# Transposes moved from TensorE to DMA and more GELU chunks on VectorE, in a fused attention and MoE kernel

## The chip, the cores and the metric

The kernel runs on one core of a Trainium2 chip. Its engines are TensorE (PE in the profile; its weight loads are PEld), ScalarE (ACT), VectorE (DVE), GpSimd (POOL) and SyncE (SP), which here only issues DMAs. The metric is the device time of one execution in microseconds, as the median of several runs. Lower is better.

## The reference

Two stages, one after the other, for B = 4 batches, 12288 queries each, C = 128 channels:

```python
kv_pool = kv.reshape(B, H // 4, 4, W // 4, 4, C).mean(axis=(2, 4))   # 768 pooled rows per batch
k = v = kv_pool.reshape(B, -1, C) @ w_sr
a = softmax(q @ k.T / sqrt(C))                                       # 12288 x 768 per batch
x = (a @ v).reshape(49152, 128)
h = x @ w_in                                                         # 128 -> 2048
out = (h * sigmoid(1.702 * h)) @ w_out                               # 2048 -> 128
```

Inputs and output are float32; the kernel multiplies in bfloat16 and accumulates in float32.

## The kernel before

**Units.** Queries go in groups of 512 (`G`), 96 of them (`NG`); group `i` belongs to batch `i // 24`. A batch has 768 keys, 6 chunks of 128 (`JC`). The MoE has 16 chunks of 128 hidden channels per group (`FCH`). The unit of work is a chunk: 128 keys (or hidden channels) by 512 queries.

**Two rounds.** The kernel does attention for groups 0 to 47, the first MoE for them, attention for groups 48 to 95, the second MoE. Each stage is a stream of fills and drains. A fill is up to three matmuls of 128x512 into three banks of PSUM, then one ACTIVATE over all of them (exp or GELU), which writes weights in bfloat16 into `ag`, a store of 102 chunks in SBUF. A drain multiplies stored chunks by the values (128x129 matmuls, the last column being the sum) or by `w_out` (128x512). Two sets of three banks alternate between fills (`banks` 0, 1, 2 and 3, 4, 5); banks 6 and 7 (`acc`) serve everything else: accumulators of drains, transposes, keys, single chunks.

**A planner orders everything.** The code runs a list of fills (`seq`) with a list of drains (`todo`) and places drains and extra jobs between fills by a model of time in units of one 512-column matmul (`COST`, `now`, `end`, `dve`). The result is a fixed order of instructions on each engine; each engine runs in order and waits on semaphores. `background(i)` and `background_moe(g)` are called when the first fill of a group is prepared, up to two fills ahead of the drains that stand beside it, and issue loads and stores that belong to that moment. `extras` is a queue of small jobs that the planner fits in.

**Chunks on VectorE.** Some chunks skip ScalarE: `early_fill` makes one 128x512 matmul into bank 6 or 7 and VectorE computes exp or GELU by a polynomial and, for GELU, a reciprocal, into `aside` (three slots in rotation). `rolling` names the exp chunks, `lent` the GELU chunks, `early` four groups (48 to 51) whose 24 exp chunks are made during the first MoE. `raw`, a float32 copy of the chunk that GELU needs, lives in one of the four buffers of `qT`.

```python
rolling = [(i, JC - 1) for i in [10, *range(38, NG // R, 6), *range(57, 90, 6)]]
lent = [(g, FCH - 1) for g in range(52, 94) if g % 5 in (2, 4)]
```

That is 9 exp chunks beside the 24 early ones, and 17 GELU chunks, all in the second MoE.

**Queries.** Groups 0 to 11 are loaded with a cast into SBUF (`load_q`, on POOL's queue), and TensorE transposes them, four 128x128 transposes per group (`transpose_q`, L236), with a copy by VectorE (L242). All others are cast to DRAM (`cast_q`, POOL) and read back transposed by DMA (`load_qT`, SP), 2048 queries at a time.

**Keys and values.** Batches 0 and 1 are pooled by TensorE in the first attention stage. Batches 2 and 3 are pooled by eight pairs of accumulating DMAs (`add_kv`, POOL), started at groups 2 to 9 and 24 to 31 of the first MoE. Then, for each half `a` of a batch, at groups 12 and 14 (34 and 36), `use_kv` adds the last two terms on VectorE (`sum_kv`) and queues three jobs: `transpose_pooled` (four 96-row transposes on TensorE, L184, and a copy, L186), `make_k` (one 384-column matmul, L192, and a copy) and `make_v` (three 128-column matmuls, L199, and a copy, L201).

**Queues.** SP carries, in this order of mention only, the transposed query reads, the put-away of attention results to DRAM (`put_away`, 768 KB or 2 x 384 KB), their transposed return (`bring_back`), and the outputs (`out_dram<-o_sb`, four DMAs of 64 KB per group). `x`, `qT` and `o_sb` names in the profile are these tiles; `o_sb` has three buffers.

Of the kernel before, what the change touches and what calls it, by code (L numbers as in the profile page):

```python
# [7 lines left out]
F32 = mybir.dt.float32  # L8
# [16 lines left out]
def kernel(  # L25
# [23 lines left out]
    q_flat = q.rearrange("b n c -> (b n) c")  # L49
    x_bf = nc.dram_tensor("x_bf", (B * N, C), BF, kind="Internal").ap()  # L50
    q_bf = nc.dram_tensor("q_bf", (B * N, C), BF, kind="Internal").ap()

    kv_r = kv.rearrange("b (ch p) (a w) c -> b a ch p (w c)", p=128, a=2)

# [65 lines left out]
    def new_keys(b):  # L120
        kTs[b] = kvres.tile([128, J], BF, name="kT")

        vs[b] = kvres.tile([128, JC, C + 8], BF, name="v")
        nc.vector.memset(vs[b][:, :, C:C + 1], 1.0)

    def load_chunk(b, jc):
# [51 lines left out]
        pooled[b, a] = kvtmp.tile([Hp, 4, C], BF, name="pooled")  # L178
        nc.vector.tensor_tensor(pooled[b, a], t[:, 0], t[:, 1], ADD)

    def transpose_pooled(b, a):
        ps = acc_bf()[:, 0:h].rearrange("p (a b) -> p a b", a=4)
        for wp in range(4):
            nc.tensor.transpose(ps[:, wp, :], pooled[b, a][:, wp, :], ident[:Hp, :Hp])  # L184
        pTs[b, a] = kvtmp.tile([128, h], BF, name="pT")
        nc.vector.tensor_copy(pTs[b, a], ps.rearrange("p a b -> p (a b)"))  # L186

    def make_k(b, a):
        ps = acc()
        if a == 0:  # L190
            new_keys(b)
        nc.tensor.matmul(ps[:, :h], w_sr_sb, pTs[b, a], start=True, stop=True)  # L192
        nc.vector.tensor_copy(kTs[b][:, a * h:(a + 1) * h], ps[:, :h])

    def make_v(b, a):
        ps = acc()
        pT = pTs.pop((b, a))
        for k in range(K):
            nc.tensor.matmul(ps[:, k * C:(k + 1) * C], pT[:, k * 128:(k + 1) * 128], w_sr_sb,  # L199
                             start=True, stop=True)  # L200
        nc.vector.tensor_copy(vs[b][:, a * K:(a + 1) * K, 0:C], ps[:, :h].rearrange("p (k c) -> p k c", k=K))  # L201
        for jc in range(a * K, a * K + K):
            vs[b, jc] = True

    qTs = {}

    def cast_q(s):
        sl = slice(s * SG, (s + 1) * SG)
        nc.gpsimd.dma_start(out=q_bf[sl, :].rearrange("(p i) c -> p (i c)", p=128),
                            in_=q_flat[sl, :].rearrange("(p i) c -> p (i c)", p=128))  # L210

    def load_qT(s):
        qTs[s] = qpool.tile([128, 1, SG], BF, name="qT")
        nc.vector.memset(qTs[s][:, 0, 0:1], 0.0)
        nc.sync.dma_start_transpose(out=qTs[s], in_=q_bf[s * SG:(s + 1) * SG, :])


    QS = 3
    qs = [x_tile(XS - 1 - JC - s) for s in range(QS)]
# [8 lines left out]
    def transpose_q(g):  # L228
        s = g // 4
        turned.add(g)  # L230
        if g % 4 == 0:
            qTs[s] = qpool.tile([128, 1, SG], BF, name="qT")
        ps = acc_bf()[:, 0:G].rearrange("p (i t) -> p i t", i=4)
        for i in range(4):
            o = (g % 4) * G + i * 128
            nc.tensor.transpose(ps[:, i, :], qs[s][:, o:o + 128], ident)  # L236
        dst = qTs[s][:, 0, (g % 4) * G:(g % 4 + 1) * G].rearrange("p (t i) -> p t i", i=4)
        src = ps.rearrange("p i t -> p t i")
        if g == 0:
            nc.scalar.copy(dst, src)  # L240
        else:
            nc.vector.tensor_copy(dst, src)  # L242
# [10 lines left out]
    for jc in range(2, JC):  # L253
        load_chunk(0, jc)
    load_q(1, 2, 4)
    for s in range(2, QS):
        load_q(s, 0, 2)
        load_q(s, 2, 4)
    cast_q(3)
    cast_q(4)  # L260

# [66 lines left out]
        return K * len(free_frames())  # L328

    early = range(NG // R, NG // R + EARLY)  # L330
    rolling = [(i, JC - 1) for i in [10, *range(38, NG // R, 6), *range(57, 90, 6)]]
    lent = [(g, FCH - 1) for g in range(52, 94) if g % 5 in (2, 4)]
    aside = agpool.tile([128, K, 512], BF, name="aside")

    def weights(c):
        if c[0] == "a" and c[1] in early:
            return ag[:, (c[1] - early[0]) * JC + c[2], :]
        if c[0] == "a" and c[1:] in rolling:
            return aside[:, rolling.index(c[1:]) % K, :]
        if c[0] == "m" and c[1:] in lent:  # L340
            return aside[:, (len(rolling) + lent.index(c[1:])) % K, :]
        return ag[:, slot_of[c], :]


# [56 lines left out]
    COEFFS = (1.0000001192092896, -0.6931469440460205, 0.24022120237350464, -0.05550713464617729, 0.009675541892647743, -0.001327647129073739)  # L401

    def early_fill(i, jc):
        nonlocal steps, raw
        ps = acc()
        if (i, jc) in lent:
            if raw is None:
                raw = qpool.tile([128, 1, SG], BF, name="qT")[:, 0, 0:2 * G].bitcast(F32)
            nc.tensor.matmul(ps, w_in_sb[:, jc * 128:(jc + 1) * 128],  # L409
                             x[:, i % (4 * XS) * G:(i % (4 * XS) + 1) * G], start=True, stop=True)  # L410
            steps = lent_gelu(ps, weights(("m", i, jc)))
            early_step()
            return
        rhs = qTs[i // 4][:, 0, (i % 4) * G:(i % 4 + 1) * G]
        nc.tensor.matmul(ps, kTs[i // GB][:, jc * 128:(jc + 1) * 128], rhs, start=True, stop=True)  # L415
        steps = early_exp(ps, weights(("a", i, jc)))
        early_step()

    def early_step():
        nonlocal steps  # L420
# [58 lines left out]
    raw = None  # L479
    made, used = {}, []  # L480
    steps, early_todo = None, [c for c in rolling if c[0] < early[0]]
    early_todo += [(i, jc) for i in early for jc in range(JC)]
    early_todo += [c for c in rolling if c[0] > early[-1]] + lent

    def early_fits(p, i, jc):
        if (i, jc) in rolling:
            group = seq[p][1][0][0] if seq[p][0] == "a" else seq[p][1][0][0] // (NG // R) * (NG // R) + NG // R - 1
            return (i // GB, jc) in vs and (i in turned or i // 4 in qTs and i // 4 - 1 <= group // 4 and i >= 4 * QS) and len(used) > rolling.index((i, jc)) - K
        if (i, jc) in lent:
            return seq[p][0] == "m" and seq[p][1][0][0] >= i - 2 and len(used) > len(rolling) + lent.index((i, jc)) - K  # L490
        return low and min(slot_of.values()) >= low and (2, JC - 1) in vs

    def early_waits(t):
# [26 lines left out]
        nc.vector.memset(one, 0.0)  # L520
        nc.gpsimd.memset(one, 0.0)  # L521

    TURN = {6: 3, 7: 4, 8: 5, 20: 6, 21: 7, 22: 8, 25: 9, 32: 10, 35: 11, 40: 12}
    CAST = {0: [5], 13: [6], 14: [7], 15: [8], 16: [9], 26: [10, 11], 27: [12]}
    CAST_MOE = {20: 13, 21: 14, 22: 15, 23: 16, 33: 17, 34: 18, 35: 19, 36: 20, 37: 21, 38: 22, 39: 23}

    def background(i):

        first_round = i < GB * 2
        s = TURN.get(i, NS) if first_round else i // 4 + 3 if i % 4 == 0 else NS  # L530
        if s < NS:
            load_qT(s)
        if i in CAST:
            gate()
            for s in CAST[i]:
                cast_q(s)
        if i in (10, 12):
            gate()
            for jc in range(i % 10 * 3 // 2, i % 10 * 3 // 2 + 3):
                load_chunk(1, jc)  # L540
        if 0 <= i - 16 < JC:
            extras.append((key_and_value, 1, i - 16))
        if 0 <= i - 15 < JC:
            extras.append((pool_chunk, 1, i - 15))
        if i in (28, 33, 38):
            put_away(0, (i - 28) // 5)
        if i in (31, 36, 41):
            bring_back(0, (i - 31) // 5)
        if i == 28:
            gate()  # L550
            nc.gpsimd.dma_start(out=w_in_sb, in_=moe_w_in)
        if i == 29:
            gate()
            nc.gpsimd.dma_start(out=w_out_sb, in_=moe_w_out.rearrange("(o p) c -> p o c", p=128))

    def background_moe(g):
# [4 lines left out]
        if n == 0 and FIRST <= m < RT // PART:  # L561
            (bring_back if odd else put_away)(n, m)
        g += n * 4 * XS
        nonlocal low
        if g == 12:
            low = EARLY * JC
            order[:] = [f for f in order if f >= low // K]
# [3 lines left out]
        if g in (41, 42):  # L571
            load_qT(g - 28)
        if g == 43:
            background(early[0])
        for b, lo in ((2, 2), (3, 24)):
            if lo <= g < lo + 8:
                gate()
                add_kv(b, g - lo)
            if g in (lo + 10, lo + 12):
                use_kv(b, (g - lo - 10) // 2)  # L580

    def use_kv(b, a):
        nonlocal extra_at
        sum_kv(b, a)
        on_dve(3.5)
        extra_at = max(extra_at, dve + 1.5)
        extras.extend([(transpose_pooled, b, a), (make_k, b, a), (make_v, b, a)])

    extras = []

# [120 lines left out]
    def prepare(p):  # L711
# [3 lines left out]
        for i, jc in part:  # L715
# [22 lines left out]
        15: [(pool_chunk, 0, 5)],  # L738
        16: [(key_and_value, 0, 5), (later, 6)],
        17: [(later, 7)],  # L740
        18: [(later, g) for g in range(8, 12)]}

# [1 line left out]
    FIXED, CHUNK, SWITCH, HANDOVER, EVACUATE = 0.295, 1.978, 6.0, 1.0, 4.5  # L746
    COST = {pool_chunk: (1.9, 2.6), key_chunk: (0.3, 2.4), value_chunk: (0.3, 2.4),
            transpose_q: (1.05, 4.2), early_fill: (1.0, 5.5), key_and_value: (0.55, 3.5),
            transpose_pooled: (0.9, 3.6), make_k: (0.8, 3.2), make_v: (0.8, 3.7)}
    COPY = {pool_chunk: 1.5, key_chunk: 1.5, value_chunk: 1.5, key_and_value: 2.8, transpose_q: 3.2}  # L750
    SMALL = 0.26
    RECIPROCAL = 8.2
# [44 lines left out]
    for n in range(len(seq)):  # L797
        fill(n + 2)
        jobs(n + 3)
        while True:  # L800
# [13 lines left out]
            if f:  # L814
                now = max(now, bank) + COST[f][0]
                f(*args)
                free[last_acc] = dve + 1.0 if f is early_fill else copied(f)
                if f in (transpose_pooled, make_k, make_v):
                    on_dve(2.5)
                extra_at = max(now + PAUSE, dve + 1.5 if f in (transpose_pooled, make_k, make_v) else 0.0)  # L820
                if f is early_fill:
                    pass
                else:
# [69 lines left out]
```

## Time and profile before

| | |
|---|---|
| median of 3 runs (lowest to highest) | 948.67 us (948.58 to 948.71) |
| span of the profiled execution | 946.7 us (some 2.0 us lie around it) |
| TensorE clock granted | 1.00 in all 40 slices |
| first attention, ACTIVATEs of exp | 8.7 to 141 us |
| first MoE, ACTIVATEs of GELU | 143 to 487 us |
| second attention | 488 to 604 us |
| second MoE | 605 to 942 us |
| DMA moved | 95.5 MB, 101 GB/s on average |

A row of the profile's groups names line, engine, operation, tiles out<-in and count, then the busy time and the mean of one instruction. In the windows, a number in brackets with x is the count of instructions that ran in that stretch. A bare matmul's duration includes its way through the array, which overlaps the next one's; the distance between starts is what it costs in a stream. Some matmul records are missing from the trace (6200 of 6314), weight loads are not.

### The profile page before, as it was taken

How to read it: one execution, taken by the hardware profiler on the slowest of the kernel's cores; microseconds unless marked ns; L12 is line 12 of the kernel's file. 1: busy time of each engine (PE TensorE's matmuls, PEld its weight loads, DVE VectorE, ACT ScalarE, POOL GpSimd, SP SyncE). 2: the span in 40 equal slices, each digit the busy share in tenths (PEclk: the TensorE clock that was granted, in tenths of full speed). 3: DMA queues.
4: the chain of work that ended last, by engine and by line, in shares of the span. 5: the costliest groups of instructions: out<-in, count | busy, mean ns of one | idle time of the engine just before them, and what ended most of it. 6: DMA issues, size and time to landing. Idle time of an engine off the chain costs nothing.

```text
span 946.7 us, 15374 instructions
## 1 busy us (share of the span) xinstructions
PE 933.9 (99%) x6200; PEld 502.5 (53%) x6314; DVE 575.1 (61%) x1091; ACT 933.5 (99%) x709; POOL 66.5 (7%) x115
## 2 busy tenths in 40 slices
PE   8999999999999999999999999999999999999998
PEld 4677776444444444444446777744444444444444
DVE  5753653011678776667765765376767766777651
ACT  6999999999999999999999999999999999999998
POOL 3101001330000232000000000000000000000000
PEclk9999999999999999999999999999999999999999
DMA  9997943999867799865335683552222222222222
GB/s 210 195 207 168 181 92 52 130 163 170 164 117 114 119 147 119 127 99 87 56 58 105 138 170 84 119 123 42 36 39 40 38 41 34 44 34 45 34 45 46
DMA packets 372856, 95.46 MB, mean 101 GB/s; under 512 B 346720, under 2 KB 370400, under 8 KB 372320
## 3 DMA queue, kind: packets, MB, share of 16 engines
q1 hardware_dynamic: 344000, 62.36, 36.9%
q0 software_dynamic: 28512, 31.99, 22.3%
q8 instruction: 49, 0.80, 0.3%
q14 instruction: 23, 0.19, 0.1%
q10 hardware_dynamic: 272, 0.13, 0.0%
HBM read 52.49 MB, written 48.76 MB: 107 GB/s over the span
## 4 chain that ended last, share of the span: by engine, by line
PE 97%; ACT 1%; DMA 1%; issue 1%; DVE 0%; POOL 0%; POOLq 0%
PE banks L606 35%; PE banks L596 34%; PE banks L363 14%; PE banks L350 12%; ACT ag L352 1%; PE banks L415 1%; DMA x<-in_kv_dram 1%; PE banks L139 0%; PE banks L409 0%; PE banks L634 0%; PE banks L236 0%; POOL x L222 0%; PE banks L161 0%; PE banks L294 0%; PE banks L192 0%
## 5 line engine op out<-in xcount | busy, mean ns | idle before, releaser
L598 ACT ACTIVATE ag<-banks 128x1536 bf16<-128x1536 f32 (+1 forms) x509 | 681.1, 1489 | 0.0
L596 PE MATMUL banks<-x,w_in_sb 128*128 128x512 bf16 x1476 | 405.8, 379 | 1.7
L606 PE MATMUL banks<-ag,w_out_sb 128*128 128x512 bf16 x1477 | 402.6, 379 | 1.7
L352 ACT ACTIVATE ag<-banks 128x1536 bf16<-128x1536 f32 (+2 forms) x192 | 245.6, 1421 | 3.5 <-PE banks L236 2.3
L606 PEld LDWEIGHTS <-w_out_sb 128*128 128x128 bf16 x1520 | 148.3, 98 | 177.2 <-issue 0.2
L596 PEld LDWEIGHTS <-w_in_sb 128*128 128x128 bf16 x1519 | 147.1, 98 | 171.3 <-issue 0.7
L617 DVE STREAM_TRANSPOSE o_sb<-banks 128x512 f32<-128x512 f32 x95 | 68.1, 717 | 171.4 <-PE banks L606 166.9
L363 PEld LDWEIGHTS <-ag 128*128 128x128 bf16 x2268 | 145.5, 98 | 44.6 <-issue 0.3
L363 PE MATMUL banks<-v,ag 128*128 128x129 bf16 x2268 | 163.0, 220 | 0.2
L350 PE MATMUL banks<-qT,kT 128*128 128x512 bf16 x498 | 145.0, 379 | 3.5 <-ACT ag L352 0.5
L442 DVE SCALAR_TENSOR_TENSOR ea<-ea,eb 128x512 f32<-128x512 f32 x132 | 90.4, 685 | 3.7 <-DVE ea L442 0.7
L386 DVE RECIPROCAL rec<-banks 128x3 f32<-128x3 f32 x124 | 22.3, 180 | 85.3 <-PE banks L363 84.9
L389 DVE TENSOR_TENSOR x<-banks,rec 128x384 bf16<-128x384 f32 x124 | 69.1, 557 | 4.3
L350 PEld LDWEIGHTS <-kT 128*128 128x128 bf16 x543 | 45.8, 98 | 25.9 <-issue 2.0
L473 DVE RECIPROCAL eb<-ea 128x256 f32<-128x256 f32 x34 | 57.6, 1724 | 0.5
L466 DVE SCALAR_TENSOR_TENSOR ea<-ea,eb 128x512 f32<-128x512 f32 x68 | 46.5, 683 | 1.9
L173 POOL DMA_DIRECT2D kvs<-in_kv_dram x32 | 40.4, 1323 | 19.3 <-DMA kvs<-in_kv_dram 17.1
L431 DVE TENSOR_SCALAR ea<-banks 128x512 f32<-128x512 f32 x33 | 22.8, 692 | 29.6 <-PE banks L415 29.2
L521 POOL MEMSET gate_tile<- 1x1 f32 x38 | 3.4, 89 | 325.8 <-DVE gate_tile L520 325.8
L453 DVE TENSOR_SCALAR qT<-banks 128x512 f32<-128x512 f32 x17 | 11.8, 692 | 20.7 <-PE banks L409 20.6
L437 DVE SCALAR_TENSOR_TENSOR eb<-eb,ea 128x512 f32<-128x512 f32 x33 | 22.8, 691 | 0.9
L444 DVE SCALAR_TENSOR_TENSOR ag<-ea,ee 128x512 bf16<-128x512 f32 x24 | 16.6, 691 | 1.2
(83 smaller groups left out, 286.3 us busy)
## 6 DMA issues: line engine op xcount, KB each, us to landing
out_dram<-o_sb SPq DMA_DIRECT2D x380, 64.0 KB, 2.0
kvs<-in_kv_dram POOLq DMA_DIRECT2D x32, 384.0 KB, 6.3
q_bf<-in_q_dram POOLq DMA_DIRECT2D x21, 512.0 KB, 6.6
x_bf<-x SPq DMA_DIRECT2D x13, 768.0 KB, 5.6
x<-in_kv_dram POOLq DMA_DIRECT2D x11, 512.0 KB, 10.4
x_bf<-x SPq DMA_DIRECT2D x6, 384.0 KB, 4.6
x<-in_q_dram POOLq DMA_DIRECT2D x5, 256.0 KB, 15.3
x<-in_kv_dram SPq DMA_DIRECT2D x1, 1024.0 KB, 5.0
```

The source lines that it names most:

```text
L173: nc.gpsimd.dma_start(out=kv_sums[b][:, i2], in_=kv_p[b, i, w, :, i2], **({"accum_op": ADD} if n else {}))
L350: nc.tensor.matmul(ps[:, k, :], kTs[i // GB][:, jc * 128:(jc + 1) * 128], rhs, start=True, stop=True)
L352: nc.scalar.activation(place([("a",) + c for c in chunks]), ps, AF.Exp, scale=scale)
L363: nc.tensor.matmul(av_of[u][:, k * (C + 1):(k + 1) * (C + 1)], weights(("a", i, jc))[:, o:o + T], vs[i // GB][:, jc, 0:C + 1], start=(jc = ...
L389: nc.vector.tensor_tensor(to, ps[:, :, 0:C], rec.unsqueeze(2).broadcast_to([128, TS, C]), MUL)
L442: nc.vector.scalar_tensor_tensor(a, a, COEFFS[k], b, ADD, MUL)
L466: nc.vector.scalar_tensor_tensor(a, a, COEFFS[k], b, ADD, MUL)
L473: nc.vector.reciprocal(b[:, m:m + 256], a[:, m:m + 256])
L596: nc.tensor.matmul(ps[:, k, :], w_in_sb[:, fc * 128:(fc + 1) * 128], x[:, g % (4 * XS) * G:(g % (4 * XS) + 1) * G], start=True, stop=True)
L598: nc.scalar.activation(place([("m",) + c for c in chunks]), ps, AF.Gelu_apprx_sigmoid)
L606: nc.tensor.matmul(o_of[g], w_out_sb[:, fc, :], weights(("m", g, fc)), start=(fc == 0), stop=(fc == FCH - 1))
L617: nc.vector.transpose(o_sb, o_of.pop(g))
```

## The change

It does four things.

1. Queries of groups 10 and 11 are cast to DRAM (`cast_q(2, 2)`, in the place of their load) and read back transposed by DMA (`load_rest`, issued at group 5) instead of being transposed on TensorE.
2. For batches 2 and 3, the pooled halves are written to DRAM (`put_pooled`) and read back transposed (`turn_pooled`); `make_k` stays on TensorE; the values are the transposed keys, so keys are written to DRAM (`put_k`) and read back transposed into `v` (`turn_k`, three DMAs of 128x128 per half). `transpose_pooled` and `make_v` go. The steps are two groups apart. Batch 2 starts at group 0 instead of 2; the sum comes 9 (and 10) groups after the start instead of 10 and 12.
3. 24 GELU chunks instead of 17 are made by VectorE, six of them in the first MoE (groups 3, 6, 8, 9, 13, 14) before the early exp chunks, 18 in the second; 10 exp chunks of `rolling` instead of 9, in other groups.
4. `raw` is taken at group 40 of the first attention and returned at group 43; query tile 12 is loaded at group 42 instead of 40. The rows of `v` are 8 elements wider.

```diff
-        vs[b] = kvres.tile([128, JC, C + 8], BF, name="v")
+        vs[b] = kvres.tile([128, JC, C + 16], BF, name="v")
...
-    def transpose_pooled(b, a):
...
-    def make_v(b, a):
...
+    def put_pooled(b, a):
+        nc.sync.dma_start(out=pool_bf[b, a].rearrange("w h c -> h w c"), in_=pooled[b, a])
+
+    def turn_pooled(b, a):
+        pTs[b, a] = kvtmp.tile([128, 1, h], BF, name="pT")
+        nc.sync.dma_start_transpose(out=pTs[b, a], in_=pool_bf[b, a].rearrange("w h c -> (w h) c"))
+
+    def put_k(b, a):
+        jc = slice(a * K, a * K + K)
+        nc.sync.dma_start(out=k_bf[b, jc].rearrange("j c t -> c j t"),
+                          in_=kTs[b][:, a * h:(a + 1) * h].rearrange("c (j t) -> c j t", t=128))
+
+    def turn_k(b, a):
+        for jc in range(a * K, a * K + K):
+            nc.sync.dma_start_transpose(out=vs[b][:, jc:jc + 1, 0:C], in_=k_bf[b, jc])
...
+    def load_rest(s, lo):
+        qTs[s] = qpool.tile([128, 1, SG], BF, name="qT")
+        nc.vector.memset(qTs[s][:, 0, lo * G:lo * G + 1], 0.0)
+        nc.sync.dma_start_transpose(out=qTs[s][:, :, lo * G:], in_=q_bf[s * SG + lo * G:(s + 1) * SG, :])
...
-    for s in range(2, QS):
-        load_q(s, 0, 2)
-        load_q(s, 2, 4)
+    load_q(2, 0, 2)
+    cast_q(2, 2)
...
-    rolling = [(i, JC - 1) for i in [10, *range(38, NG // R, 6), *range(57, 90, 6)]]
-    lent = [(g, FCH - 1) for g in range(52, 94) if g % 5 in (2, 4)]
+    rolling = [(i, JC - 1) for i in (10, 29, 39, 44, 52, 61, 65, 73, 80, 90)]
+    lent = [(g, FCH - 1) for g in (3, 6, 8, 9, 13, 14, 53, 54, 57, 59, 62, 64, 66, 67, 71, 73, 75, 78, 80, 84, 86, 88, 91, 93)]
+    turn = [("a",) + c for c in rolling if c[0] < early[0]] + [("m",) + c for c in lent if c[0] < early[0]]
+    turn += [("a",) + c for c in rolling if c[0] > early[-1]] + [("m",) + c for c in lent if c[0] > early[-1]]
...
-        for b, lo in ((2, 2), (3, 24)):
+        for b, lo in ((2, 0), (3, 24)):
             if lo <= g < lo + 8:
                 gate()
                 add_kv(b, g - lo)
-            if g in (lo + 10, lo + 12):
-                use_kv(b, (g - lo - 10) // 2)
+            for a in range(2):
+                step = g - lo - 9 - a
+                if step == 0:
+                    sum_kv(b, a)
+                    on_dve(3.5)
+                    put_pooled(b, a)
+                if step == 2:
+                    turn_pooled(b, a)
+                if step == 4:
+                    extras.append((make_k, b, a))
+                if step == 6:
+                    put_k(b, a)
+                if step == 8:
+                    turn_k(b, a)
```

More of the change, by code (lines that the diff above doesn't have):

```diff
@@ L51 @@
     q_bf = nc.dram_tensor("q_bf", (B * N, C), BF, kind="Internal").ap()
+    pool_bf = nc.dram_tensor("pool_bf", (B, 2, r, Hp, C), BF, kind="Internal").ap()
+    k_bf = nc.dram_tensor("k_bf", (B, JC, C, 128), BF, kind="Internal").ap()
     kv_r = kv.rearrange("b (ch p) (a w) c -> b a ch p (w c)", p=128, a=2)
@@ L179, in sum_kv @@
         nc.vector.tensor_tensor(pooled[b, a], t[:, 0], t[:, 1], ADD)
-    def transpose_pooled(b, a):
[L182 to L186, printed above, removed]
+    def put_pooled(b, a):
[10 more added lines that the diff above has]
+            nc.sync.dma_start_transpose(out=vs[b][:, jc:jc + 1, 0:C], in_=k_bf[b, jc])
     def make_k(b, a):
@@ L191, in make_k @@
             new_keys(b)
-        nc.tensor.matmul(ps[:, :h], w_sr_sb, pTs[b, a], start=True, stop=True)
+        nc.tensor.matmul(ps[:, :h], w_sr_sb, pTs.pop((b, a))[:, 0, :], start=True, stop=True)
         nc.vector.tensor_copy(kTs[b][:, a * h:(a + 1) * h], ps[:, :h])
-    def make_v(b, a):
[L196 to L201, printed above, removed]
         for jc in range(a * K, a * K + K):
@@ L205, with cast_q @@
     qTs = {}
-    def cast_q(s):
-        sl = slice(s * SG, (s + 1) * SG)
+    def cast_q(s, lo=0):
+        sl = slice(s * SG + lo * G, (s + 1) * SG)
         nc.gpsimd.dma_start(out=q_bf[sl, :].rearrange("(p i) c -> p (i c)", p=128),
@@ L230, in transpose_q @@
         turned.add(g)
-        if g % 4 == 0:
+        if s not in qTs:
             qTs[s] = qpool.tile([128, 1, SG], BF, name="qT")
@@ L337, in weights @@
             return ag[:, (c[1] - early[0]) * JC + c[2], :]
[L338 to L341, printed above, removed]
+        if c in turn:
+            return aside[:, turn.index(c) % K, :]
         return ag[:, slot_of[c], :]
@@ L403, in early_fill @@
     def early_fill(i, jc):
-        nonlocal steps, raw
+        nonlocal steps
         ps = acc()
@@ L407, in early_fill @@
             if raw is None:
-                raw = qpool.tile([128, 1, SG], BF, name="qT")[:, 0, 0:2 * G].bitcast(F32)
+                new_raw()
             nc.tensor.matmul(ps, w_in_sb[:, jc * 128:(jc + 1) * 128],
@@ L417, in early_fill, with new_raw @@
         early_step()
+    def new_raw():
+        nonlocal raw
+        raw = qpool.tile([128, 1, SG], BF, name="qT")[:, 0, 0:2 * G].bitcast(F32)
     def early_step():
@@ L481 @@
     steps, early_todo = None, [c for c in rolling if c[0] < early[0]]
+    early_todo += [c for c in lent if c[0] < early[0]]
     early_todo += [(i, jc) for i in early for jc in range(JC)]
-    early_todo += [c for c in rolling if c[0] > early[-1]] + lent
+    early_todo += [c for c in rolling + lent if c[0] > early[-1]]
     def early_fits(p, i, jc):
@@ L487, in early_fits @@
             group = seq[p][1][0][0] if seq[p][0] == "a" else seq[p][1][0][0] // (NG // R) * (NG // R) + NG // R - 1
-            return (i // GB, jc) in vs and (i in turned or i // 4 in qTs and i // 4 - 1 <= group // 4 and i >= 4 * QS) and len(used) > rolling.index((i, jc)) - K
+            return (i // GB, jc) in vs and (i in turned or i // 4 in qTs and (i // 4 - 1 <= group // 4 if i >= 4 * QS else i - 2 <= group)) and len(used) > turn.index(("a", i, jc)) - K
         if (i, jc) in lent:
-            return seq[p][0] == "m" and seq[p][1][0][0] >= i - 2 and len(used) > len(rolling) + lent.index((i, jc)) - K
+            return seq[p][0] == "m" and seq[p][1][0][0] >= i - 2 and len(used) > turn.index(("m", i, jc)) - K
         return low and min(slot_of.values()) >= low and (2, JC - 1) in vs
@@ L521, in gate @@
         nc.gpsimd.memset(one, 0.0)
-    TURN = {6: 3, 7: 4, 8: 5, 20: 6, 21: 7, 22: 8, 25: 9, 32: 10, 35: 11, 40: 12}
+    TURN = {6: 3, 7: 4, 8: 5, 20: 6, 21: 7, 22: 8, 25: 9, 32: 10, 35: 11, 42: 12}
     CAST = {0: [5], 13: [6], 14: [7], 15: [8], 16: [9], 26: [10, 11], 27: [12]}
@@ L532, in background @@
             load_qT(s)
+        if i == 5:
+            load_rest(2, 2)
         if i in CAST:
@@ L548, in background @@
             bring_back(0, (i - 31) // 5)
+        if i == 40:
+            new_raw()
         if i == 28:
@@ L563, in background_moe @@
         g += n * 4 * XS
-        nonlocal low
+        nonlocal low, raw
         if g == 12:
@@ L573, in background_moe @@
         if g == 43:
+            raw = None
             background(early[0])
-        for b, lo in ((2, 2), (3, 24)):
+        for b, lo in ((2, 0), (3, 24)):
             if lo <= g < lo + 8:
@@ L578, in background_moe @@
                 add_kv(b, g - lo)
-            if g in (lo + 10, lo + 12):
-                use_kv(b, (g - lo - 10) // 2)
[L582 to L587, printed above, removed]
+            for a in range(2):
[12 more added lines that the diff above has]
+                    turn_k(b, a)
     extras = []
@@ L740 @@
         17: [(later, 7)],
-        18: [(later, g) for g in range(8, 12)]}
+        18: [(later, 8), (later, 9)]}
     FIXED, CHUNK, SWITCH, HANDOVER, EVACUATE = 0.295, 1.978, 6.0, 1.0, 4.5
@@ L748 @@
             transpose_q: (1.05, 4.2), early_fill: (1.0, 5.5), key_and_value: (0.55, 3.5),
-            transpose_pooled: (0.9, 3.6), make_k: (0.8, 3.2), make_v: (0.8, 3.7)}
+            make_k: (0.8, 3.2)}
     COPY = {pool_chunk: 1.5, key_chunk: 1.5, value_chunk: 1.5, key_and_value: 2.8, transpose_q: 3.2}
@@ L817 @@
                 free[last_acc] = dve + 1.0 if f is early_fill else copied(f)
-                if f in (transpose_pooled, make_k, make_v):
+                if f is make_k:
                     on_dve(2.5)
-                extra_at = max(now + PAUSE, dve + 1.5 if f in (transpose_pooled, make_k, make_v) else 0.0)
+                extra_at = max(now + PAUSE, dve + 1.5 if f is make_k else 0.0)
                 if f is early_fill:
```

## The prediction

> **What bounds the kernel now.** I read the page's busy row first and the chain second.
>
> ```profile
> PE 933.9 (99%) x6200; PEld 502.5 (53%) x6314; DVE 575.1 (61%) x1091; ACT 933.5 (99%) x709; POOL 66.5 (7%) x115
> PE 97%; ACT 1%; DMA 1%; issue 1%; DVE 0%; POOL 0%; POOLq 0%
> ```
>
> Two engines look full, so busy time doesn't decide; the chain names TensorE. Its busy time has modelled ends, so the next step is the spacing of its instructions, from the timeline (start, duration of the merged row, count).
>
> ```profile
> 27.73 0.39 PE L236 MATMUL banks<-ident,x 128*128 128x128 bf16 x4
> 28.39 0.67 PE L363 MATMUL banks<-v,ag 128*128 128x129 bf16 x9
> 229.06 0.34 PE L184 MATMUL banks<-ident,pooled 96*128 96x96 bf16 x4
> 229.23 0.81 PE L596 MATMUL banks<-x,w_in_sb 128*128 128x512 bf16 x3
> 231.56 0.33 PE L199 MATMUL banks<-w_sr_sb,pT 128*128 128x128 bf16 x3
> ```
>
> A row's length is n-1 spacings and one last duration (379 ns for 512 columns, 220 for 129, 219 for 128, 205 for 96). So 512 columns take (810-379)/2 = 215.6 ns, 129 take 56.7, 128 take 55.6, 96 take 42. With these I made a ledger of TensorE: 3650 matmuls of 512 (786.9 us), 2304 of 129 (130.6), 148 of 128 (8.2), 16 of 96 (0.7), 4 of 384 (0.6), 192 of 32 columns (4.9, 25.5 each): 932.0 us of a span of 946.7. Where the missing 14.7 lie is seen from weight loads, one per matmul, which are recorded nearly without holes (matmuls are not).
>
> ```profile
> core 0: us, PE busy (x) PEld busy (x) DVE busy (x) ACT busy (x) POOL busy (x), PEclk, DMA share, GB/s
> 24.00:36.00 12.00, 11.48 (x122) 7.75 (x121) 10.07 (x27) 11.81 (x13) 0.00 (x0) 1.00 1.07 210
> 650.00:700.00 50.00, 49.79 (x230) 22.67 (x232) 34.99 (x50) 50.00 (x38) 0.00 (x0) 1.00 0.24 37
> ```
>
> In the second MoE 232 loads x 215.6 ns = 50.0 of 50 us: TensorE is full to the last slot. Adding the ledger up to each ACTIVATE and setting it against that one's start gives its standstill: 4.5 us at the first ACTIVATE, 10.2 at number 48 (which starts at 62.9 us), 11.5 at the last (941.0). So nearly all idle time is made before 63 us, where few chunks are in stock, and after the last matmul (943.4) only 3.3 us of copies and output follow. From 63 us on, TensorE work is time, one for one; the clock column is 1.00 throughout.
>
> ScalarE has the lighter ledger. Its three-chunk ACTIVATEs follow each other at 1.331 us undisturbed, two-chunk ones at 0.907: 662 and 37 of them, with 4 table loads of 1.28 and small items, are some 922 us.
>
> **The change, part by part.** Sums are against the span of 946.7 us; 2.0 us lie around it up to the median of 948.67.
>
> *Pooled keys and values, batches 2 and 3.* The order of instructions loses 16 transposes of 96 columns (16 x 42 ns = 0.67 us) and 12 value matmuls of 128 (12 x 55.6 = 0.67). All lie in the first MoE, where TensorE is full: -1.34 us. The Trainium skill, "TensorE: Matmul & The Clock Gate", Part 4: PE-mode transpose, has a transpose at about 275 ns inside a kernel, because it waits for SBUF; these rows show 42 to 56 in a stream. By its price these 16 and the next 8 would save 6.6 us instead of 1.1.
>
> *Queries of groups 10 and 11.* Eight transposes leave: 8 x 55.6 = 0.45 us. They stand between 28 and 33 us, where TensorE is not full. The chain there runs through ScalarE in pieces:
>
> ```profile
> 29.75 3.55 ACT ag L352 x4
> 33.39 1.98 ACT ag L352 x2
> ```
>
> In the changed order, TensorE's ledger up to the same ACTIVATE 48 is 53.33 us instead of 52.75: the eight are gone, and about 18 attention matmuls of 129 columns have moved ahead of it (18 x 56.7 - 445 = 0.58 us). ScalarE's ledger up to there is the same. If ScalarE sets the pace, TensorE arrives at the same time with 0.58 us more done, and its standstill shrinks by that, on top of the 0.45; if it doesn't, only the 0.45 count. I take 0.45 of the 0.58, since ACT is busy 11.81 of the 12 us there. Bounds: 0 and 0.9 (the 0.38 us that one pool matmul at 58.1 waits for VectorE may go too).
>
> *ScalarE.* 24 chunks of GELU on VectorE instead of 17, 10 late exp chunks instead of 9: four three-chunk ACTIVATEs fewer, two two-chunk ones more, -4 x 1.331 + 2 x 0.907 = -3.51 us. TensorE's matmuls for these chunks stay. Nobody waits for ScalarE after 63 us, so I cost this at nothing. If it were the bound, it would be worth the 3.5.
>
> *VectorE.* A GELU chunk sums over its rows (13 elementwise ones of 0.42 to 0.69 us, two RECIPROCALs of 1.72) to 11.1 us, an exp chunk to 6.1. Added: 7 x 11.1 + 6.1 = 84 us; removed: eight copies of pooled tiles and two of queries, 5 us. VectorE goes from 61% to 69%. The six early chunks start 11 to 16 ACTIVATEs apart, as the 17 do in the second MoE today, where the 650 to 700 row shows VectorE at 35 of 50 us and no gap on TensorE. So they are covered; without cover each would hold the drain of its group's sixteenth chunk.
>
> *New DMAs.* Queries: a cast takes the place of a load in the Pool queue (that load is issued at 11.3 and lands 15.3 later, at 26.6), then a transpose of 1024 rows on SP. The row `qT<-q_bf` below has 4.2 us for 2048 rows, and the first of them held SP for 4.8, so it lands at 31 to 36; the first use, an exp chunk after ACTIVATE 28, is at about 37. The next transpose slips by at most 4.8 us to 41 and is first used at about 45. Covered, thinly; a microsecond beyond costs one.
>
> ```profile
> x_bf<-x SPq DMA_DIRECT2D x13, 768.0 KB, 5.6
> qT<-q_bf SPq DMA_TRANSPOSE x21, 4.2
> x<-x_bf SPq DMA_TRANSPOSE x16, 7.4
> ```
>
> Pooled: each half is put to DRAM, two groups (14.3 us) later turned, two later multiplied by `make_k`, two later put, two later turned into v. A 98 KB transpose is not in the trace: between 2.0 (an output of 64 KB) and 7.4 us (8 times its size, behind others). The values have time: the first matmul that reads them stands 26 ACTIVATEs (35 us) after `turn_k`. The keys don't: TensorE executes in order, and everything queued behind `make_k` waits with it. The first half has 14.3 us for a 768 KB put (5.6) and its own transpose (at most 7.4). The second has one buffer with the first, so SP issues it only after the first `make_k`, five ACTIVATEs (6.7 us) before its own. I take 4.2 us, the row nearest in kind, and so no stall; the worst is 7.4 plus a bring-back in front of it. While SP waits there, the outputs behind it wait too: three `o_sb` buffers, one used per 7.2 us, cover some 14 us. `turn_pooled`'s sum on VectorE comes two groups after the last accumulating load instead of three; that load lands in 6.3 us, so it is not late. The Trainium skill, "DMA: Bandwidth & Descriptors", Rules for kernel authors, speaks against this: transfers under 64 KB are mostly overhead, to be coalesced, and the twelve v transposes are 32 KB each. No run here shows one; by its fixed 2.0 us they would take 24 us of queue, all off TensorE's path.
>
> *Moved.* The batch 2 loads start two groups earlier, into a stretch (125 to 150 us) with a DMA share of 0.12. The load of query tile 12 goes from group 40 to 42, 100 us ahead of its use. At the end 64 matmuls instead of 44 follow the last fill; the ledger is the same: nothing.
>
> Sum: -1.34 - 0.45 - 0.45 + 0.1 (small waits around four new `make_k` waits; 0 to 1.5) = -2.14. From 946.7 to 944.5; the time 946.5 us.
>
> **The rivals.** What a measurement can tell from no change is about 0.2%, 1.9 us.
> - Start gives nothing: TensorE's own waits set the pace before 63 us, so only the 1.34 of the MoE and part of the 0.45 count, and the new waits take a few tenths back: 947.4. For it: in the 24 to 36 window neither engine is full. Against: the chain's ACT pieces.
> - Late keys (slower): the second half's transpose lands after TensorE has reached `make_k`. It decides from 6.7 us after the first `make_k`. With a bring-back (7.4) in front of 4.2 it takes 11.6, a stall of 4.9 in batch 2; in batch 3, without bring-backs but with query casts, a stall of about 1: -2.1 + 5.9 = +3.8, 952.5. For it: SP holds 3.4 us on a bring-back just there, and the put before it can be slow when loads run beside it. Against: the bring-back is issued some 5 us before, and a transpose of a fifth the size of qT's should be short.
> - ScalarE was the real bound: -3.5 us, 945.1. Against: 232 loads in 50 us.
>
> **How the numbers follow.** The forecast's case 0.54, its own range 945.6 to 946.8 (start 0.9 and no wait; start 0.1). The empty start 0.28, late keys 0.12, ScalarE 0.06. Faster by over 0.2% (under 946.8): 0.54 + 0.06 = 0.60. Within: 0.29, the empty start with a stall of one or two us. Slower: 0.11. The range reaches from 945.2 to 948.2: it takes in the empty start with its waits and leaves out the late keys.
>
> **What would show it.** Right: the ledger falls to 930.2; a window of the second MoE still holds 232 loads; standstill at ACTIVATE 48 near 9.6; no wait of TensorE for `pT`. Wrong: a row of weight loads waiting for a DMA at `make_k`; ScalarE gaps that come with TensorE gaps in the first MoE, where an early GELU chunk is late; or a standstill after 63 us over 2 us.

## The result and the profile after

The changed kernel takes 946.99 us (median; 946.79 to 947.40), the kernel before 948.57 us (948.33 to 948.75): 1.58 us less, a ratio of 0.9985 with a 95% interval of 0.9979 to 0.9991. The time is 0.5 us above the forecast and inside its range; it is 0.2 us short of the 946.8 from which the prediction called it faster, and so falls to its "within" (0.29).

The page of the profiled execution (span 945.2), busy row and chain:

```profile
PE 938.2 (99%) x6278; PEld 500.8 (53%) x6278; DVE 651.3 (69%) x1197; ACT 930.4 (98%) x707; POOL 66.6 (7%) x115
PE 98%; DMA 1%; ACT 0%; DVE 0%; POOL 0%; issue 0%; POOLq 0%
```

ScalarE lost 3.1 us of busy time, VectorE gained 76 (worked out: 79), and TensorE has the chain to itself. The windows of the start and of the second MoE, columns as before:

```profile
core 0: us, PE busy (x) PEld busy (x) DVE busy (x) ACT busy (x) POOL busy (x), PEclk, DMA share, GB/s
24.00:36.00 12.00, 11.69 (x131) 8.00 (x127) 9.58 (x27) 11.81 (x13) 0.00 (x0) 1.00 1.08 209
650.00:700.00 50.00, 50.00 (x234) 22.62 (x233) 39.89 (x55) 50.00 (x38) 0.00 (x0) 1.00 0.22 38
```

The second MoE is as full as before (233 loads). The start took 127 loads instead of 121 in its 12 us. The waits of TensorE for other engines (total, times, longest) hold none for `pT` and none for a value transposed by DMA:

```profile
PE banks L301 <- DVE col L273: 1.0, 1, 1.0
PE banks L141 <- DMA x<-in_kv_dram: 0.5, 1, 0.5
PE banks L357 <- ACT ag L359: 0.5, 2, 0.3
PE banks L141 <- DVE x L291: 0.4, 1, 0.4
PE banks L357 <- DVE kT L165: 0.4, 1, 0.4
PE banks L141 <- DVE x L396: 0.2, 1, 0.2
PE banks L357 <- DVE kT L151: 0.2, 1, 0.2
```

The new DMAs (count, KB, median from issue to landing):

```profile
pool_bf<-pooled SPq DMA_DIRECT2D x4, 96.0 KB, 4.5
...
v<-k_bf SPq DMA_TRANSPOSE x12, 2.4
...
pT<-pool_bf SPq DMA_TRANSPOSE x4, 5.3
```

With the prediction's method the span divides into TensorE's ledger, its standstill up to 940 us, and the tail (span less the two): before 932.23 + 10.94 + 3.51, after 930.45 + 11.00 + 3.74. The ledger fell by the 1.78 worked out (with the prediction's rounded prices it is 932.0 and 930.2); standstill and tail gave 0.3 back, where the prediction had 0.35 more to gain from them.

### The profile page after: what moved, and what is told of

It reads as the page before. It is cut to its first block, busy times and chain, and to the rows that moved or that the text cites. A ratio compares the mean times of both kernels' runs of the same rounds, so it can differ in the third digit from the quotient of the medians.

```text
span 945.2 us, 15545 instructions
## 1 busy us (share of the span) xinstructions
PE 938.2 (99%) x6278; PEld 500.8 (53%) x6278; DVE 651.3 (69%) x1197; ACT 930.4 (98%) x707; POOL 66.6 (7%) x115
## 4 chain that ended last, share of the span: by engine, by line
PE 98%; DMA 1%; ACT 0%; DVE 0%; POOL 0%; issue 0%; POOLq 0%
PE banks L628 35%; PE banks L618 35%; PE banks L370 14%; PE banks L357 12%; PE banks L422 1%; DMA x<-in_kv_dram 1%; PE banks L416 1%; PE banks L141 0%; ACT ag L359 0%; PE banks L656 0%; POOL x L230 0%; PE banks L163 0%; PE banks L244 0%; PE banks L301 0%; PE banks L203 0%
## 5 line engine op out<-in xcount | busy, mean ns | idle before, releaser
L357 PE MATMUL banks<-qT,kT 128*128 128x512 bf16 x542 | 148.3, 379 | 1.3 <-ACT ag L359 0.5
L453 DVE SCALAR_TENSOR_TENSOR ea<-ea,eb 128x512 f32<-128x512 f32 x136 | 93.2, 686 | 3.8 <-DVE ea L453 0.6
L484 DVE RECIPROCAL eb<-ea 128x256 f32<-128x256 f32 x48 | 81.8, 1725 | 0.8
L477 DVE SCALAR_TENSOR_TENSOR ea<-ea,eb 128x512 f32<-128x512 f32 x96 | 65.7, 685 | 2.6
L464 DVE TENSOR_SCALAR qT<-banks 128x512 f32<-128x512 f32 x24 | 16.6, 692 | 26.2 <-PE banks L416 26.2
```

What stands on the lines that cost most here:

```text
L357: nc.tensor.matmul(ps[:, k, :], kTs[i // GB][:, jc * 128:(jc + 1) * 128], rhs, start=True, stop=True)
L453: nc.vector.scalar_tensor_tensor(a, a, COEFFS[k], b, ADD, MUL)
L477: nc.vector.scalar_tensor_tensor(a, a, COEFFS[k], b, ADD, MUL)
L484: nc.vector.reciprocal(b[:, m:m + 256], a[:, m:m + 256])
```

## The experiments

Line numbers are each kernel's own. "Before" was measured again beside each set, at 948.40 to 948.47; the changed kernel was measured in the first set alone, at 946.99.

### The parts, each alone

`kv_only` has the pooled keys and values by DMA, `q_only` the queries, `lists_only` the new chunk lists, `no_lists` both DMA moves with the old lists. Against the changed kernel the edits are these, alone or together (with the old lists, the handling of `raw` and of query tile 12 goes back too):

```diff
 # old lists
-    rolling = [(i, JC - 1) for i in (10, 29, 39, 44, 52, 61, 65, 73, 80, 90)]
-    lent = [(g, FCH - 1) for g in (3, 6, 8, 9, 13, 14, 53, ...)]
+    rolling = [(i, JC - 1) for i in [10, *range(38, NG // R, 6), *range(57, 90, 6)]]
+    lent = [(g, FCH - 1) for g in range(52, 94) if g % 5 in (2, 4)]
 # queries of groups 10 and 11 on TensorE
-    cast_q(2, 2)
+    load_q(2, 2, 4)
-        if i == 5:
-            load_rest(2, 2)
-        18: [(later, 8), (later, 9)]}
+        18: [(later, g) for g in range(8, 12)]}
 # batches 2 and 3 on TensorE: transpose_pooled, make_k, make_v as before
```

> The kernel before with only the keys and values of batches 2 and 3 moved to DMA. Ledger theory (after the start TensorE is full, so its work is time one for one and relief of ScalarE is worth nothing): its TensorE ledger is 1.34 us shorter, so 947.2, at most 0.3 more for waits at make_k. ScalarE theory (the fewer ACTIVATEs made the gain): no change, 948.6.

> The kernel before with only the queries of groups 10 and 11 moved to DMA. Ledger theory: the ledger is 0.45 us shorter, but it lies in the start, where standstill may take its place: between 0 and -0.45, 948.1 to 948.6. My prediction had -0.9 for this part (948.1 would be half of it, 947.7 all). ScalarE theory: no change.

> The kernel before with only the new lists of VectorE's chunks (24 GELU, 10 late exp, six of the GELU in the first MoE) and the buffer that goes with them. TensorE's ledger is the same, ScalarE's 3.5 us shorter. Ledger theory: no change, 948.6 within 0.2. ScalarE theory: the whole gain, 947.0 or less.

> The changed kernel with the lists of the kernel before: both moves to DMA, 17 GELU chunks. TensorE's ledger is that of the changed kernel, ScalarE's that of the kernel before. Ledger theory: as the changed kernel, 947.0 within 0.2. ScalarE theory: as the kernel before, 948.6.

Measured: `kv_only` 948.17 (ratio 0.9997, 0.9988 to 1.0006), `q_only` 949.18 (1.0007, 0.9998 to 1.0016), `lists_only` 949.29 (1.0008, 0.9999 to 1.0017), `no_lists` 948.74 (1.0003, 0.9994 to 1.0012). No part gains alone by more than its interval, and the two DMA moves together gain nothing with the old lists, though TensorE's ledger falls by the full 1.78 us. This contradicts the step "TensorE work is time, one for one" as it stood, and also the rival in which ScalarE alone is the bound: its relief alone gains nothing either.

Where the 1.78 us went in `no_lists` is seen in its chain, which now names ScalarE, and at its end. The chain, one of TensorE's waits and its timeline:

```profile
ACT 94%; PE 4%; DMA 1%; issue 0%; DVE 0%; POOL 0%; ACTq 0%; POOLq 0%
PE banks L653 <- ACT ag L617: 0.6, 1, 0.6
```

```profile
928.66 0.81 PE L625 MATMUL banks<-ag,w_out_sb 128*128 128x512 bf16 x3
929.36 0.81 PE L615 MATMUL banks<-x,w_in_sb 128*128 128x512 bf16 x3
930.01 0.81 PE L625 MATMUL banks<-ag,w_out_sb 128*128 128x512 bf16 x3
930.70 0.81 PE L615 MATMUL banks<-x,w_in_sb 128*128 128x512 bf16 x3
```

Three fill matmuls (L615) take turns with three drain matmuls (L625). From fills to drains there are 0.65 us, from drains to fills 0.69 to 0.70: TensorE waits 51 ns before every fill and moves at ScalarE's pace, 1.34 us for three chunks. Then it waits 0.6 us in the last drain. `kv_only` has the same wait there, 0.3 us (`PE banks L651 <- ACT ag L615`); in the changed kernel there is none.

How close the two engines are is seen where they end. The last matmuls and the last ACTIVATEs, of the kernel before:

```profile
940.78 2.62 PE L634 MATMUL banks<-w_out_sb,ag 128*128 128x128 bf16 x44
937.29 4.77 ACT L598 ACTIVATE ag<-banks 128x1024 bf16<-128x1024 f32 x5
```

and of `no_lists`:

```profile
942.10 0.95 PE L653 MATMUL banks<-w_out_sb,ag 128*128 128x128 bf16 x14 [0.63 <-ACT ag L617]
937.36 4.68 ACT L617 ACTIVATE ag<-banks 128x1024 bf16<-128x1024 f32 x5
```

In `no_lists`, where TensorE waits, its last matmul ends 1.01 us after ScalarE's last ACTIVATE (943.05 and 942.04). `kv_only` has the same 1.01, and so have both kernels of the next experiment. In the kernel before it is 1.34 (943.40 and 942.06): TensorE could become 0.33 us faster there before it had to wait for ScalarE. In `lists_only` ScalarE ends 3.4 us earlier (938.63), and TensorE 5.78 us after it. In the changed kernel the distance is 2.55 (941.67 and 939.12).

This gave a second theory. Call the chunks that ScalarE has finished and TensorE has not yet read the stock (ACTIVATE ends, three, two or one chunk each, less the weight loads that read them; the 24 chunks that VectorE makes into the same buffer are added back). In the kernel before it is 38 to 40 at 80 us, goes down and up with the stages, and in the second MoE only down, from over 20 at 650 us. While there is stock, TensorE's work is time. Once it is gone, TensorE can only keep ScalarE's pace, and its own lighter work is worth nothing. Near 900 us the stock is some 10 chunks before, 14 after, 6 in `kv_only`, 2 in `no_lists` (a working minimum), 27 in `lists_only`.

### ScalarE's relief taken away

```diff
-    lent = [...]
+    lent = []
```

in the changed kernel (`after_nolent`, with the handling of query tile 12 and the early `raw` as before) and in the kernel before (`before_nolent`).

> The changed kernel without the 24 GELU chunks on VectorE: all of them go back to ScalarE. TensorE's ledger stays at 930.45 us. ScalarE's ledger rises from 912.1 to 922.8 us of ACTIVATEs (+10.65). Theory one, TensorE's work alone is the time (the prediction's): 947.0, within half a microsecond. Theory two, both engines are full after 63 us and the later of the two ends sets the time: in the changed kernel ScalarE's last ACTIVATE ended at 939.1 us and TensorE's last matmul at 941.7; with 10.65 us more ScalarE ends at 949.8, about 1.0 us of drain follows on TensorE, and the time is 955.5 to 956.5.

> The kernel before without its 17 GELU chunks on VectorE. TensorE's ledger stays at 932.23 us, ScalarE's rises from 915.65 to 923.2 us (+7.56). Theory one, TensorE alone: 948.6. Theory two, the later of two ends: ScalarE's last ACTIVATE ended at 942.06, so now at 949.6, with 1.0 us of drain behind it, 955.5 to 956.5. Under theory two this kernel and the changed one without VectorE's GELU differ by their ScalarE ledgers alone (0.4 us), although TensorE has 1.78 us more to do here; under theory one they differ by 1.6.

Measured: 955.81 us (955.52 to 955.99; ratio 1.0077, 1.0061 to 1.0092) and 955.62 (955.35 to 955.70; 1.0075, 1.0061 to 1.0089). Theory two had 955.5 to 956.5 for both. The kernel with 1.78 us more TensorE work is no slower than the other. One window of `after_nolent` early and one late in the second MoE:

```profile
650.00:700.00 50.00, 49.79 (x229) 22.64 (x232) 5.02 (x7) 50.00 (x38) 0.00 (x0) 1.00 0.25 43
890.00:940.00 50.00, 49.68 (x220) 21.60 (x223) 5.02 (x7) 50.00 (x39) 0.00 (x0) 1.00 0.21 36
```

At 650 us this ScalarE-bound kernel shows the same 232 loads on which the prediction rested. Its stock runs out at about 720 us (in `before_nolent` at about 760), and from there a window holds 223 or 224: six matmuls per 1.344 us. The page of `before_nolent` names the other engine in its chain:

```profile
ACT 96%; PE 2%; DMA 1%; issue 1%; POOL 0%; DVE 0%; ACTq 0%; POOLq 0%
```

### TensorE's work added

```diff
-        nc.tensor.matmul(ps[:, :h], w_sr_sb, pTs.pop((b, a))[:, 0, :], start=True, stop=True)
+        pT = pTs.pop((b, a))
+        for _ in range(5):
+            nc.tensor.matmul(ps[:, :h], w_sr_sb, pT[:, 0, :], start=True, stop=True)
```

> The changed kernel with make_k's matmul issued five times over: 16 matmuls of 384 columns more, TensorE's ledger +2.59 us at 162 ns each, spread over four places between 234 and 411 us; nothing else differs. TensorE alone: 946.99 + 2.6 = 949.6. Two engines: in the changed kernel ScalarE is ready 1.5 us before TensorE at the end, so TensorE is the later one and the time is 949.6 too. If ScalarE set the time of the changed kernel, it would stay at 947.0.

Measured: 949.33 us (949.13 to 949.63), +2.34 against the changed kernel for +2.59 of ledger. So in the changed kernel, with some 14 chunks in stock at 900 us, TensorE's work is time at nearly its full price.

### The whole with one part undone

`lists_kv` leaves the queries on TensorE, `lists_q` the pooled keys and values; `no_six` drops the first six of the new GELU list:

```diff
-    lent = [(g, FCH - 1) for g in (3, 6, 8, 9, 13, 14, 53, ...)]
+    lent = [(g, FCH - 1) for g in (53, ...)]
```

> The changed kernel with the queries of groups 10 and 11 turned on TensorE again; lists and pooled keys as changed. TensorE's ledger 930.89 us (+0.45 against the changed kernel), ScalarE's 912.14 of ACTIVATEs, as changed. TensorE alone, and two engines with TensorE the later one: 946.99 + 0.45 = 947.4, less if the eight transposes lie in idle time (947.0). If the query DMA does harm, as its run alone hinted (+0.7): 946.3.

> The changed kernel with batches 2 and 3 pooled keys and values on TensorE again; lists and queries as changed. TensorE's ledger 931.79 us (+1.34 against the changed kernel), ScalarE's 912.14. Both theories have TensorE as the later one here: 946.99 + 1.34 = 948.3; if the small waits of the new lists (+0.5 in the run of the lists alone) come with the old pooled chain, up to 948.9.

> The changed kernel without the six GELU chunks in the first MoE (18 in the second stay). TensorE's ledger 930.45 us as changed; ScalarE's 914.80 of ACTIVATEs, +2.66. TensorE alone: 947.0. Two engines: ScalarE's last ACTIVATE ended at 939.1 in the changed kernel and TensorE at 941.7, with about 1.0 us of drain behind ScalarE, so ScalarE has 1.5 us to spare; 2.66 - 1.5 = 1.1 us more: 948.1. It lies between the changed kernel (0) and the one with both DMA moves and the old lists (+3.51 on ScalarE, 948.74).

Measured: `lists_q` 948.93 us (1.0014, 0.9998 to 1.0030), +1.94 for an expected 1.3 to 1.9; ten of its eleven executions lie between 948.70 and 949.31, one took 958.11, and why is not known. `lists_kv` 948.96 (1.0005, 0.9996 to 1.0014), +1.97 where 0.45 was expected. `no_six` 951.99 (1.0037, 1.0025 to 1.0049), +5.0 where theory two had 1.1. So the later of two ends is not all of it either. The timeline of TensorE in `no_six` (in brackets the idle time before a row and what ended it):

```profile
748.10 0.38 PE L628 MATMUL banks<-aside,w_out_sb 128*128 128x512 bf16 x1
748.32 0.81 PE L618 MATMUL banks<-x,w_in_sb 128*128 128x512 bf16 x3
749.51 0.81 PE L618 MATMUL banks<-x,w_in_sb 128*128 128x512 bf16 x3 [0.38 <-ACT ag L620]
...
753.54 0.81 PE L618 MATMUL banks<-x,w_in_sb 128*128 128x512 bf16 x3 [0.54 <-ACT ag L620]
```

Fifteen fill matmuls, five fills of three, stand in a row, with no drain between, and each threesome after the first waits for ScalarE to free its banks. A shorter row of nine stands at 656.71. The order is written when the kernel is built: the planner starts no drains of a group whose VectorE chunk is not finished by its modelled clock, and fills on instead. Each row begins after the last drain of a group and ends where the next group's drains begin, so I read them as that rule; it was not tried by itself. The stock grows by some 10 chunks at the long row, TensorE's standstill goes from 10.93 us at 650 to 15.20 at 800 (some 1.6 of it at the short row, 2.6 at the long one), and some 22 chunks are left in stock at 900, which TensorE must still drain when ScalarE is done. `lists_kv` has one such row of nine fill matmuls at 501.55:

```profile
501.55 0.81 PE L357 MATMUL banks<-qT,kT 128*128 128x512 bf16 x3
502.73 0.81 PE L357 MATMUL banks<-qT,kT 128*128 128x512 bf16 x3 [0.37 <-ACT ag L359]
504.08 0.81 PE L357 MATMUL banks<-qT,kT 128*128 128x512 bf16 x3 [0.54 <-ACT ag L359]
```

Its standstill rises by 1.74 us between 500 and 550 us, against 0.22 in the changed kernel: this, and 0.44 of ledger, is its loss. In the orders of the changed kernel and of the other kernels above no more than six fill matmuls stand in a row. So, by this reading, with both moves in place the new lists keep VectorE's chunks on time by the planner's clock; with the queries undone, or the six early chunks left out, they don't.

### Late keys

```diff
-                if step == 2:
+                if step == 4:
                     turn_pooled(b, a)
```

> The changed kernel with each transpose of pooled keys issued two groups (14.3 us) later, in the same step that queues its make_k. In the changed kernel make_k ran at 234.3, 240.5, 404.5 and 411.2 us and the transposes landed 2.4 to 6.4 us after their issue. Issued at about 231.1, 238.3, 403.8 and 411.1 they land 0 to 3.2, 0 to 4.2, 1.7 to 5.7 and 2.3 to 6.3 us too late: 4 to 19 us of waits, some 9. If TensorE's standstill is time one for one: 951 to 966. If the chunks in stock absorb it (both engines have slack after all): 947 to 948.

Measured: 973.70 us (967.84 to 974.77; ratio 1.0254, 1.0228 to 1.0279), well beyond the upper end; the profile is of the fastest execution. Its waits and timeline:

```profile
PE banks L203 <- DMA pT<-pool_bf: 17.0, 4, 8.8
```

```profile
241.65 0.50 PE L203 MATMUL banks<-pT,w_sr_sb 128*128 128x384 bf16 x1 [7.07 <-DMA pT<-pool_bf]
241.94 1.49 PE L618 MATMUL banks<-x,w_in_sb 128*128 128x512 bf16 x3
243.22 0.63 PE L628 MATMUL banks<-ag,w_out_sb 128*128 128x512 bf16 x1
...
244.50 0.93 PE L618 MATMUL banks<-x,w_in_sb 128*128 128x512 bf16 x3
...
246.13 0.81 PE L618 MATMUL banks<-x,w_in_sb 128*128 128x512 bf16 x3
```

The stall is time, one for one, and more. The transposes themselves were short (2.5 to 4.4 us). They waited in SP's queue: the first was issued at 237.19 us instead of the assumed 231.1, behind outputs and two puts, and the second at 255.63, behind outputs of the stalled TensorE and a bring-back that held SP for 3.8 us. The rest of the extra time of this execution is in the hardware section below.

### A further step in the same direction

`v1_dma` also turns batch 1's values by DMA (`key_only` makes the keys alone):

```diff
-            extras.append((key_and_value, 1, i - 16))
+            extras.append((key_only, 1, i - 16))
+        if i == 23:
+            put_k(1, 0)
+            put_k(1, 1)
+        if i == 24:
+            turn_k(1, 0)
+            turn_k(1, 1)
```

> The changed kernel with batch 1's values, too, turned by DMA from its keys: six value matmuls of 128 columns fewer between 54 and 70 us, two puts and six transposes on SP more. TensorE's ledger 930.12 us (-0.33); ScalarE's as changed, and with 1.5 us to spare. Both theories: 946.7 if the six lie where TensorE is full, 947.0 if they lie in idle time; over 947.3 if the transposes delay a query transpose or a bring-back on SP.

Measured: 954.0 us (952.78 to 957.15; ratio 1.0066, 1.0053 to 1.0078). That is far over the 947.3 from which a delay on SP was expected to show, and what came late were the values themselves. The waits of TensorE:

```profile
PE banks L375 <- DMA v<-k_bf: 4.7, 2, 3.3
```

the window around them, and the first fill after them:

```profile
84.00:100.00 16.00, 11.31 (x127) 8.16 (x126) 7.13 (x19) 11.45 (x9) 2.18 (x5) 0.89 1.04 119
```

```profile
99.51 1.49 PE L362 MATMUL banks<-qT,kT 128*128 128x512 bf16 x3
```

The last two 32 KB transposes took 15.5 and 15.8 us to land (issued 82.32 and 83.60), in a stretch with a DMA share of 1.04; in the changed kernel their like took 2.4. The waits are not the whole loss of 7 us: behind them TensorE ran at half pace until about 103.4 us (1.49 us for three matmuls instead of 0.81), which costs some 2 more. What slowed the two transposes is not shown; four others had been issued just before them, and a transpose of 2048 query rows, issued next, held SP for 12.1 us.

## Why the prediction was right or wrong

*Ledger, -1.78:* right. It is 930.45 us, and in the changed kernel TensorE work is time (+2.34 for +2.59). The 275 ns with which the prediction compares is how long one transpose takes; the like here is 205 to 219 ns, and what left with each was the distance between starts, 42 to 56.

*Start, -0.45 beyond the eight transposes:* mis-sized. From 10 to 63 us the standstill grows by 4.63 us before and by 4.41 after; over the fourteen kernels of this case it is 4.40 to 4.63 with the query transposes by DMA (4.40 to 4.54 in all but one) and 4.62 to 4.76 without. So some 0.2 came, at the lower end of the bounds of 0 to 0.9. It did not last: between 63 and 155 us the changed kernel's standstill grew by 0.32, before by 0.07, with a pause of 0.14 us at 140.3 where the first MoE begins; the kernels with the new list of exp chunks show 0.2 to 0.3 there (`v1_dma`, which stalls, aside).

*Small waits, +0.1:* measured nearer to +0.5, inside the bounds of 0 to 1.5. From 63 to 940 us the standstill grows by 1.35 us, before by 1.12, and the tail is 0.23 longer. One pause is where the prediction put it, 0.16 us behind a `make_k` at 240.5.

*"Nobody waits for ScalarE after 63 us, so I cost this at nothing":* this step failed. As a reading of the profile it was true of both kernels. As a price it was wrong: with both DMA moves but the old lists the time is 948.74, so with the moves in place the lists are worth 1.75 us, more than the whole gain. What the step left out is that in the kernel before TensorE was only 0.33 us of work from having to wait for ScalarE. Neither the forecast's theory nor the rival "ScalarE was the real bound" holds. The two engines are matched, and a full TensorE window shows only that the stock lasts until then. So that the total came within 0.5 us is partly luck: the forecast paid the gain to TensorE's lighter work alone, and it came because the change brings ScalarE's relief along. The Trainium skill, "Perfetto Trace Analysis", Identifying the Most-Contended Engine, would optimize the engine of highest occupancy first, and doesn't take matmul busy time as TensorE's measure. Here TensorE's ledger fills 98% of the span and ScalarE is busy for 99%, and either one's relief alone moved the time by -0.3 to +0.8 us.

*Pooled chain by DMA:* right. The transposes of 98 KB took 2.4 to 6.4 us (taken: 4.2) and landed 12.0, 3.5, 8.7 and 1.2 us before their `make_k`. The last is closest, as the prediction feared for second halves. The twelve of 32 KB landed in 2.3 to 4.1 us, and no matmul waited for them. The rival "late keys" did not come. Its own delay was not tried; `late_keys`, which issues the transposes 14.3 us late, shows its mechanism and that the price of a stall grows: the waits were 17.0 us where some 9 were expected, as SP's queue and TensorE hold each other up, and the span 20.9 us longer (the median time 27).

*Queries by DMA:* covered. The transpose landed at 35.5 (31 to 36 expected), with 8.8 us for half of the rows that took 4.2.

*Open:* why `q_only` and `lists_only` lose 0.7 and 0.8 us although TensorE's ledger does not rise. Their standstills are 0.5 above the kernel before's, in many pauses of 0.1 to 0.2 us, and the rest is in the tail; no single wait carries it.

## What to carry to other kernels

Where two engines are both at 98%, price a relief of either by the stock between them: follow finished but unread chunks along the span, see which engine it runs out for, and when, and compare where the two engines end. A full window of one engine early in a stage doesn't say that the other has time to spare at its end. Where a planner writes the order, a part measured alone is a part under another order, so look for long rows of one kind of instruction before reading such a run as the part's price.

## What the runs showed of the hardware

- After a wait of 7 or 9 us TensorE ran at half its pace for a while. In `late_keys` three matmuls of 512 columns at 241.94 are 430 ns apart ((1.49 - 0.63) / 2), and from about 245.3 us on 216 again; the window from 240 to 250 us has a granted clock of 0.76. Twice 3.6 us at half pace cost 3.6 us on top of the 17.0 of waits, which is the rise in standstill (20.5). The Trainium skill, "TensorE: Matmul & The Clock Gate", Part 1, states that an idle array drops to half clock and needs about 3.4 us of work to return; this trace agrees.
- The same 32 KB transpose by DMA takes 2.4 us in a quiet stretch and 15.8 with a DMA share of 1.04, and one of 256 KB took 8.8 in the busy start (share 1.08).
- ScalarE's own pace is 1.342 to 1.344 us for a three-chunk ACTIVATE rather than the 1.331 of the undisturbed spacing: more than half follow at 1.331, others 10, 20 or 60 ns later, in all fourteen kernels, and with ScalarE as the bound too. Over 660 of them this is 7 to 9 us, most of what looked like ScalarE's spare time in the ledger.
